# Two sets of PSUM evictions move from VectorE to ScalarE in a fused performer-attention and mixer kernel

## The chip, the cores and the metric

The kernel runs on one core of a Trainium2 chip. The metric is the device time of one execution in microseconds (us); the time before is the median of three runs. Everything about where time goes is read from one profiled execution, taken by the hardware profiler. Engines are called as in the profile: PE is TensorE, DVE is VectorE, ACT is ScalarE, POOL is GpSimd, SP is SyncE.

## The reference

Eight batches of eight heads with 576 rows of 64 go through a linear attention with random features, and its output goes through a mixer over tokens and then over channels:

```python
def phi(x):                                   # x: q or k, scaled
    h = einsum('bhsd,md->bhsm', x, omega) - sum(x * x) / 2
    return exp(h - max(h)) / sqrt(m)          # 128 features
kv  = einsum('bhsm,bhsd->bhmd', phi(k), v);  z = sum(phi(k), axis=2)
num = einsum('bhsm,bhmd->bhsd', phi(q), kv)
den = einsum('bhsm,bhm->bhs', phi(q), z) + 1e-06
x = (num / den).transpose(0, 2, 1, 3).reshape(8, 576, 512)
u = x + (relu(x.T @ w_tok1) @ w_tok2).T       # token mixing, 576 -> 256 -> 576
out = u + relu(u @ w_ch1) @ w_ch2             # channel mixing, 512 -> 1536 -> 512
```

## The kernel before

**Tiling.** The 576 rows of a batch are split into a main part of 512 rows (four blocks of 128) and a tail of 64 rows. The tails of two batches share one tile of 128 partitions: `xt[0]` and `xt[1]` hold the normalised tails of alternate pairs of batches, batch b using partitions `(b % 2) * 64` onward. In the profile the two are `xt`.

**Attention, per pair of heads (hp).** `t_main` and `t_tail` (L174, L185) transpose q and k on PE; DVE copies the result out (qT, kT at L182, tailT at L193). `q_proj` and `k_proj` (L241, L252) multiply by omega, and ACT takes the exponential out of PSUM (q_p, k_p, k_pt, q_pt, all at L197). `k_max` (L267) finds each row's maximum of k_p on DVE (mx L270, km L274, reciprocal v_sc L278) and POOL scales v with it (L279). `kv` (L286) accumulates five matmuls, and ACT casts the result to kv_sb (L301). `num` (L304) makes, for one head, a PSUM tile num_ps with five blocks of 65 columns: four main blocks and one tail block, the last column of each being the denominator. Then DVE takes the reciprocal of the denominators (rc, L317), multiplies the four main blocks into the batch's tile xm (L318), and multiplies the tail block into xt (L325).

**Token mixing.** `tok1` (L334) multiplies the four main blocks (L339) and then the shared tail tile xt (L342) by w_tok1; the half of the weight tile that belongs to the other batch of the pair is zero, so the matmul reads all of xt. Its relu is on ACT for the first half (L346) and on DVE for the second (L348). `tok2` (L350) adds the residual on DVE (um, L358), and `u_transpose` (L375) transposes the sum on PE and copies it on DVE (uT, L379).

**Channel mixing.** `ch1` (L387) makes twelve blocks of 128 channels: four matmuls (L393) and a relu into r3. Two of three relus are on ACT (L403); those of blocks 2, 5, 8 and 11 (`cb % 3 == 2`) are on DVE (L401). `ch2` (L405) accumulates twelve matmuls (L408), DVE adds the residual (o_sb, L417) and SP stores it.

**Order.** The scheduler is off: each engine runs its instructions in the order in which the program issues them, and that order is one list sorted by hand-written places (`at`, L168; `spread`, L465). A pair of heads takes one unit. Attention of batch b lies at places 4b to 4b+4, its token mixing at about 4(b+1)+0.85 to +3.85, its channel mixing at 4(b+2) to 4(b+3). So three batches are in flight, and channel mixing begins when two batches of attention are done. Within a unit, the relus of `ch1` and the exponentials stand in one queue on ACT, and the work of `k_max`, `num`, `tok2`, `u_transpose` and `ch2` in one queue on DVE. `num` of a pair stands behind `k_max` of the next pair.

**Buffers.** PSUM has eight banks: five for attention tiles (`att_ps`) and three for the mixer's (`mix_ps`). A matmul that opens a tile waits until the bank's former tile has been read.

Of the kernel before, what the change touches and what calls it, by code (L numbers as in the profile page):

```python
# [11 lines left out]
AF = mybir.ActivationFunctionType  # L12
ALU = mybir.AluOpType
# [4 lines left out]
def kernel(  # L18
# [17 lines left out]
    nc = tc.nc  # L36

    B, H, S, D = q.shape
# [6 lines left out]
    ST = S - SM  # L45
    NJ = SM // P
# [14 lines left out]
    def att_ps(shape, dt, name):  # L61
        return pspool.tile(shape, dt, name=name, tag="attps", bufs=5)

    def mix_ps(shape, dt, name):
        return pspool.tile(shape, dt, name=name, tag="mixps", bufs=3)
# [105 lines left out]
    live = {}  # L171
# [132 lines left out]
    def num(b, hp, i):  # L304
        h = 2 * hp + i
        if h == 0:
            live["x", b] = mpool.tile([P, NJ, DM], FP16, name="xm", tag="xm")
        sb = live["kv", b, h]
        ps = att_ps([P, NJ + 1, D + 1], FP32, "num_ps")
        for j in range(NJ):  # L310
            nc.tensor.matmul(  # L311
                ps[:, j, :], live["qp", b, hp][:, j % 2, 2 * i + j // 2, :], sb, start=True, stop=True
            )
        c0 = ST + (h % 2) * 256 + hp * ST - (b % 2) * ST
        nc.tensor.matmul(ps[:, NJ, :], q_pt[b % 2][:, c0 : c0 + P], sb, start=True, stop=True)
        rc = apool.tile([P, NJ + 1], FP32, name="rc", tag="rc")
        nc.vector.reciprocal(out=rc, in_=ps[:, :, D])  # L317
        nc.vector.tensor_tensor(  # L318
            out=live["x", b][:, :, h * D : (h + 1) * D],
            in0=ps[:, 0:NJ, 0:D],  # L320
            in1=rc[:, 0:NJ].unsqueeze(2).broadcast_to((P, NJ, D)),
            op=ALU.mult,
        )
        r0 = (b % 2) * ST
        nc.vector.tensor_scalar(  # L325
            out=xt[(b // 2) % 2][r0 : r0 + ST, h * D : (h + 1) * D],
            in0=ps[r0 : r0 + ST, NJ, 0:D],
            scalar1=rc[r0 : r0 + ST, NJ : NJ + 1],
            scalar2=None,
            op0=ALU.mult,  # L330
        )


# [53 lines left out]
    def ch1(c, cb):  # L387
        if cb == 0:
            live["r3", c] = mpool.tile([P, NCB, SM], FP16, name="r3", tag="r3")
        uT = live["uT", c] if c < B else uTt  # L390
        ps = mix_ps([P, SM], FP32, "h3_ps")
        for db in range(ND):
            nc.tensor.matmul(  # L393
                ps,
                wc1[:, db, cb * P : (cb + 1) * P],
                uT[:, db].rearrange("p j c -> p (j c)"),
                start=(db == 0),
                stop=(db == ND - 1),
            )
        if cb % 3 == 2:  # L400
            nc.vector.tensor_relu(out=live["r3", c][:, cb, :], in_=ps)  # L401
        else:
            nc.scalar.activation(out=live["r3", c][:, cb, :], in_=ps, func=AF.Relu)  # L403

    def ch2(c, j):  # L405
        ps = mix_ps([P, DM], FP32, "h2_ps")
# [35 lines left out]
    for b in range(B):  # L442
        g = 4 * b
        at(g - 0.95, t_main, b, 0, "q")
        at(g - 0.80, t_main, b, 0, "k")
        at(g - 0.45, t_tail, b)
        at(g - 0.20, q_tail, b)
        at(g + 0.40, k_tail, b, 0)
        at(g + 0.50, k_tail, b, 1)
        at(g + 0.70, k_tail_max, b)  # L450
        at(g + 1.02, t_main, b, 1, "q")
        at(g + 1.70, t_main, b, 1, "k")
        for hp in range(NU):
            u = g + hp
            at(u + 0.04, q_proj, b, hp, 0)
            at(u + 0.10, q_proj, b, hp, 1)
            at(u + 0.18, k_proj, b, hp, 0)
            at(u + 0.26, k_proj, b, hp, 1)
            at(u + 0.55, k_max, b, hp)
            at(u + 1.32, kv, b, hp, 0)  # L460
            at(u + 1.40, kv, b, hp, 1)
            at(u + 1.58, num, b, hp, 0)
            at(u + 1.66, num, b, hp, 1)
# [18 lines left out]
    for c in range(B + 1):  # L482
        items = [(4, ch1, c, cb) for cb in range(NCB)] + [(12, ch2, c, j) for j in range(NJ)]
        spread(4 * (c + 2), 4 * (c + 3), items)
# [33 lines left out]
```

## Time and profile before

| | |
|---|---|
| three runs | 357.69, 357.98 and 358.46 us, median 357.98 |
| the profiled execution | 357.74 us, of which the span from first to last instruction is 355.9 us |
| PE | 314.9 us busy, 88% of the span |
| DVE | 215.7 us busy, 61%, 523 instructions |
| ACT | 138.1 us busy, 39%, 297 instructions |
| POOL | 88.8 us busy, 25% |
| granted TensorE clock | 0.987 of full speed, mean |

The span falls into three parts. Up to about 61 us there is attention of two batches, with PE busy little more than half of the time. From 61 to 281 us come six stages of about 36 us, one per batch of channel mixing, with attention, token mixing and channel mixing interleaved and PE nearly always busy. From 281 us on there is little but channel mixing left. A line of a group gives engine, line, what is written from what, the count, and after the bar the busy time, the mean duration in ns and the idle time before. A row of the stretches gives the stretch, its length, and then per engine busy time with the number of instructions, the granted clock and the DMA's share.

### The profile page before, as it was taken

What the parts mean: (1) busy time and instruction counts of PE and PEld (TensorE: products, weight loads), DVE (VectorE), ACT (ScalarE), POOL (GpSimd) and SP (SyncE); (2) the same over time, 40 slices, a digit from 0 to 9 for tenths busy, and PEclk for the clock granted to TensorE, in tenths of its full rate; (3) what the DMA queues carried; (4) which work ended last, traced back from release to release, by engine and by line L of the source; (5) the groups of instructions that cost most, each with busy time, mean ns of one, the idle gap of its engine ahead of it and who ended that gap; (6) DMA issues with size and microseconds to landing.
All of it is one profiled execution on the core that took longest, in us unless ns stands there. A gap on an engine that the chain in (4) does not pass through costs nothing.

```text
span 355.9 us, 5929 instructions
## 1 busy us (share of the span) xinstructions
PE 314.9 (88%) x2337; PEld 171.8 (48%) x2337; DVE 215.7 (61%) x523; ACT 138.1 (39%) x297; POOL 88.8 (25%) x106
## 2 busy tenths in 40 slices
PE   2546784999999998999999989999999899999994
PEld 1334352555654564556554645555545444444441
DVE  3457788377767685777676857776767645322221
ACT  1325742553265226532653256425642140040410
POOL 8787362125013500261126112111211100000000
PEclk9999998799999999999999999999999999999998
DMA  7999999009700960099009900011001100201113
GB/s 72 164 191 210 205 192 188 10 0 145 146 30 2 148 141 29 3 112 177 30 2 115 174 29 2 15 47 62 0 2 59 61 0 29 88 3 62 58 29 89
DMA packets 45916, 27.78 MB, mean 78 GB/s; under 512 B 14144, under 2 KB 40640, under 8 KB 45888
## 3 DMA queue, kind: packets, MB, share of 16 engines
q0 software_dynamic: 40640, 17.96, 40.3%
q1 hardware_dynamic: 5248, 9.44, 7.6%
q8 instruction: 18, 0.29, 0.3%
q14 instruction: 10, 0.08, 0.1%
HBM read 35.91 MB, written 9.44 MB: 127 GB/s over the span
## 4 chain that ended last, share of the span: by engine, by line
PE 68%; DVE 20%; POOL 3%; issue 3%; DMA 3%; ACT 2%; DVEq 0%; ACTq 0%; POOLq 0%
PE h_ps L393 26%; PE h_ps L408 21%; PE k_ps L258 3%; DVE xm L318 3%; DVE km L274 3%; PE h_ps L339 3%; PE ht_ps L355 3%; PE q_ps L247 3%; DMA w1m<-in_moe_w_tok_dram 3%; PE t_ps L180 2%; DVE xt L325 2%; DVE mx L270 2%; DVE uT L379 2%; PE kv_ps L290 2%; DVE um L358 2%
## 5 line engine op out<-in xcount | busy, mean ns | idle before, releaser
L393 PE MATMUL h_ps<-uT,wc 128*128 128x512 f16 x384 | 95.9, 384 | 7.3 <-DVE uT L379 7.2
L408 PE MATMUL h_ps<-wc,r 128*128 128x512 f16 x432 | 98.1, 379 | 0.5 <-DVE ut L373 0.3
L279 POOL TENSOR_TENSOR v_sc<-v_nat,v_sc 128x512 f16<-128x512 f16 x32 | 34.0, 1062 | 168.2 <-DVE rc L317 103.1
L403 ACT ACTIVATE r<-h_ps 128x512 f16<-128x512 f32 x72 | 43.1, 598 | 79.8 <-PE h_ps L393 79.8
L393 PEld LDWEIGHTS <-wc 128*128 128x128 f16 x432 | 40.3, 98 | 50.0 <-issue 13.2
L408 PEld LDWEIGHTS <-r 128*128 128x128 f16 x432 | 41.3, 98 | 46.2 <-issue 1.1
L401 DVE TENSOR_SCALAR r<-h_ps 128x512 f16<-128x512 f32 x36 | 24.8, 690 | 58.7 <-PE h_ps L393 58.5
L197 ACT ACTIVATE q_p<-q_ps 128x512 f16<-128x512 f32 x64 | 37.0, 595 | 50.6 <-PE q_ps L247 49.9
L197 ACT ACTIVATE k_p<-k_ps 128x512 f16<-128x512 f32 x64 | 37.9, 602 | 26.4 <-PE k_ps L258 26.4
L417 DVE TENSOR_TENSOR o_sb<-um,h_ps 128x512 f32<-128x512 f16 x32 | 21.9, 684 | 38.4 <-PE h_ps L408 38.2
L318 DVE TENSOR_TENSOR xm<-num_ps,rc 128x256 f16<-128x256 f32 x64 | 27.2, 424 | 2.2
L258 PE MATMUL k_ps<-bd,kT 128*128 128x256 f16 x128 | 25.6, 291 | 0.7 <-ACT q_p L197 0.3
L247 PE MATMUL q_ps<-qT,bd 128*128 128x512 f16 x64 | 24.4, 407 | 0.0
L358 DVE TENSOR_TENSOR um<-xm,ht_ps 128x512 f16<-128x512 f16 x32 | 21.8, 681 | 2.0 <-PE ht_ps L355 1.5
L274 DVE TENSOR_REDUCE km<-mx 128x8 f16<-128x512 f16 x32 | 22.0, 686 | 1.1
L258 PEld LDWEIGHTS <-kT 128*128 128x128 f16 x128 | 12.9, 104 | 16.6 <-issue 3.5
L311 PEld LDWEIGHTS <-q_p 128*128 128x128 f16 x256 | 15.3, 98 | 10.5 <-issue 4.0
L290 PEld LDWEIGHTS <-k_p 128*128 128x128 f16 x256 | 14.2, 101 | 12.5 <-issue 8.2
L290 PE MATMUL kv_ps<-v_sc,k_p 128*128 128x65 f16 x256 | 15.4, 197 | 5.3 <-POOL v_sc L279 5.1
L355 PE MATMUL ht_ps<-r,w2m 128*128 128x512 f16 x64 | 19.0, 379 | 0.1
L311 PE MATMUL num_ps<-kv_sb,q_p 128*128 128x65 f16 x256 | 17.3, 194 | 1.9 <-ACT kv_sb L301 1.7
L325 DVE TENSOR_SCALAR xt<-num_ps,rc 64x64 f16<-64x64 f32 x64 | 17.8, 279 | 0.5
(81 smaller groups left out, 363.4 us busy)
## 6 DMA issues: line engine op xcount, KB each, us to landing
out_dram<-o_sb SPq DMA_DIRECT2D x32, 256.0 KB, 2.3
v_nat<-in_v_dram POOLq DMA_DIRECT2D x8, 512.0 KB, 10.4
q_nat<-in_q_dram POOLq DMA_DIRECT2D x7, 512.0 KB, 5.9
k_nat<-in_k_dram POOLq DMA_DIRECT2D x7, 512.0 KB, 8.4
wc<-in_moe_w_ch_dram POOLq DMA_DIRECT2D x2, 1536.0 KB, 18.2
out_dram<-o_sb SPq DMA_DIRECT2D x8, 128.0 KB, 2.3
qk_tail<-in_q_dram POOLq DMA_DIRECT2D x8, 64.0 KB, 8.0
qk_tail<-in_k_dram POOLq DMA_DIRECT2D x8, 64.0 KB, 8.2
```

The costliest lines, as they stand in the source:

```text
L197: nc.scalar.activation(out=out, in_=in_, func=AF.Exp, bias=0.0, scale=c_scale)
L247: nc.tensor.matmul(ps, bd[:, w * M : (w + 1) * M], sb[:, i0 : i0 + 4, :], start=True, stop=True)
L258: nc.tensor.matmul(ps[:, 2 * pr : 2 * pr + 2, :], sb[:, (hp % 2) * 4 + 2 * i + pr, :], bd, start=True, stop=True,)
L274: nc.vector.reduce_max(out=mx, in_=tmp, axis=AX.X)
L279: nc.gpsimd.tensor_tensor(out=vs[:, :, 0:D], in0=nat["v", b][:, 2 * hp : 2 * hp + 2, :].rearrange("p h (j d) -> p (h j) d", d=D), in1=vs[: ...
L290: nc.tensor.matmul(ps, live["kp", b, hp][:, i, j, :], live["vsc", b, hp][:, i * 4 + j, 0 : D + 1], start=(j == 0), stop=False,)
L311: nc.tensor.matmul(ps[:, j, :], live["qp", b, hp][:, j % 2, 2 * i + j // 2, :], sb, start=True, stop=True)
L318: nc.vector.tensor_tensor(out=live["x", b][:, :, h * D : (h + 1) * D], in0=ps[:, 0:NJ, 0:D], in1=rc[:, 0:NJ].unsqueeze(2).broadcast_to((P, ...
L355: nc.tensor.matmul(ps, w2m[:, tb, j, :], live["r1", b][:, tb, :], start=(tb == 0), stop=(tb == NT - 1))
L393: nc.tensor.matmul(ps, wc1[:, db, cb * P : (cb + 1) * P], uT[:, db].rearrange("p j c -> p (j c)"), start=(db == 0), stop=(db == ND - 1),)
L403: nc.scalar.activation(out=live["r3", c][:, cb, :], in_=ps, func=AF.Relu)
L408: nc.tensor.matmul(ps, live["r3", c][:, cb, j * P : (j + 1) * P], wc2[:, cb, :], start=(cb == 0), stop=(cb == NCB - 1),)
```

## The change

Two evictions from PSUM change engine. In `num`, the multiplication of the tail block by the reciprocal (64 partitions, 64 columns, one per head, 64 in all) becomes an ACT activation with the function Copy and the reciprocal as a scale per partition. In `ch1`, the relu of every third block becomes an ACT activation like the others (four per batch and stage, nine stages, 36 in all). Nothing else is edited; places, tiles and buffers stay.

```diff
     # num(b, hp, i)
-        nc.vector.tensor_scalar(
+        nc.scalar.activation(
             out=xt[(b // 2) % 2][r0 : r0 + ST, h * D : (h + 1) * D],
-            in0=ps[r0 : r0 + ST, NJ, 0:D],
-            scalar1=rc[r0 : r0 + ST, NJ : NJ + 1],
-            scalar2=None,
-            op0=ALU.mult,
+            in_=ps[r0 : r0 + ST, NJ, 0:D],
+            func=AF.Copy,
+            scale=rc[r0 : r0 + ST, NJ : NJ + 1],
         )
     # ch1(c, cb)
-        if cb % 3 == 2:
-            nc.vector.tensor_relu(out=live["r3", c][:, cb, :], in_=ps)
-        else:
-            nc.scalar.activation(out=live["r3", c][:, cb, :], in_=ps, func=AF.Relu)
+        nc.scalar.activation(out=live["r3", c][:, cb, :], in_=ps, func=AF.Relu)
```

DVE's queue goes from 525 rows to 425. In the first place shown, DVE stands in the second stage of channel mixing, where block 8 has been multiplied and the first two heads of the next batch (num_ps 1557 and 1573) are being normalised; h3_ps is the PSUM tile of a ch1 block, h1_ps that of tok1. Before:

```order
L401 TENSOR_SCALAR r3_1373<-h3_ps_1543 128x512
L270 TENSOR_TENSOR mx_1549<-k_p_1504 128x512
L274 TENSOR_REDUCE km_1551<-mx_1549 128x8
L278 RECIPROCAL v_sc_1553<-km_1551 128x8
L317 RECIPROCAL rc_1563<-num_ps_1557 128x5
L318 TENSOR_TENSOR xm_1556<-num_ps_1557,rc_1563 128x4x64
L325 TENSOR_SCALAR xt1_110<-num_ps_1557,rc_1563 64x64
L317 RECIPROCAL rc_1579<-num_ps_1573 128x5
L318 TENSOR_TENSOR xm_1556<-num_ps_1573,rc_1579 128x4x64
L325 TENSOR_SCALAR xt1_110<-num_ps_1573,rc_1579 64x64
L182 COPY kT_1592<-t_ps_1583 128x1024
L348 TENSOR_SCALAR r1_1509<-h1_ps_1600 128x512
```

The same place on DVE now:

```order
L270 TENSOR_TENSOR mx_1549<-k_p_1504 128x512
L274 TENSOR_REDUCE km_1551<-mx_1549 128x8
L278 RECIPROCAL v_sc_1553<-km_1551 128x8
L317 RECIPROCAL rc_1563<-num_ps_1557 128x5
L318 TENSOR_TENSOR xm_1556<-num_ps_1557,rc_1563 128x4x64
L317 RECIPROCAL rc_1579<-num_ps_1573 128x5
L318 TENSOR_TENSOR xm_1556<-num_ps_1573,rc_1579 128x4x64
L182 COPY kT_1592<-t_ps_1583 128x1024
L347 TENSOR_SCALAR r1_1509<-h1_ps_1600 128x512
```

The relu ahead of the maximum and the two tail rows are gone; the rest keeps its order.

At the same place ACT has the exponentials of a pair of heads, the relu of tok1 (r_1509) and relus of ch1 (r_1373). Before:

```order
L197 ACTIVATE k_p<-k_ps 128x512
L346 ACTIVATE r_1509<-h_ps 128x512
L403 ACTIVATE r_1373<-h_ps 128x512
L197 ACTIVATE k_p<-k_ps 128x512
L301 CAST kv_sb<-kv_ps 128x65 x2
L403 ACTIVATE r_1373<-h_ps 128x512 x2
L197 ACTIVATE q_p<-q_ps 128x512 x2
```

And now:

```order
L197 ACTIVATE k_p<-k_ps 128x512
L345 ACTIVATE r_1509<-h_ps 128x512
L399 ACTIVATE r_1373<-h_ps 128x512
L197 ACTIVATE k_p<-k_ps 128x512
L301 CAST kv_sb<-kv_ps 128x65 x2
L399 ACTIVATE r_1373<-h_ps 128x512
L325 ACTIVATE xt_110<-num_ps,rc 64x64
L399 ACTIVATE r_1373<-h_ps 128x512
L325 ACTIVATE xt_110<-num_ps,rc 64x64
L399 ACTIVATE r_1373<-h_ps 128x512 x2
L197 ACTIVATE q_p<-q_ps 128x512 x2
```

The relus of blocks 8 and 11 have come in, and the two tail rows stand between relus, so that a relu behind a tail row waits for what the tail row waits for.

The last place is on ACT in the stretch before any channel mixing, where the fourth pair of heads of the first batch ends and the second batch begins (q_pt is the tail of q). Before:

```order
L197 ACTIVATE k_p<-k_ps 128x512 x2
L301 CAST kv_sb<-kv_ps 128x65 x2
L197 ACTIVATE q_pt_117<-qt_ps 128x512
L197 ACTIVATE q_p<-q_ps 128x512 x2
L197 ACTIVATE k_p<-k_ps 128x512 x2
```

And now:

```order
L197 ACTIVATE k_p<-k_ps 128x512 x2
L301 CAST kv_sb<-kv_ps 128x65 x2
L325 ACTIVATE xt_109<-num_ps,rc 64x64 x2
L197 ACTIVATE q_pt_117<-qt_ps 128x512
L197 ACTIVATE q_p<-q_ps 128x512 x2
L197 ACTIVATE k_p<-k_ps 128x512 x2
```

Two tail rows now stand ahead of the next pair's five exponentials. In the built program the tail row on ACT waits for DVE's xm (L318) of the same head, which reads the same PSUM tile, and not only for the reciprocal.

## The prediction, made before the change was run

> **What bounds the kernel now.** I read the table of stretches first, cut at the starts of the channel-mixing stages. Columns are the stretch and its length, then the busy time of PE, weight load, DVE, ACT and POOL with counts, granted clock, DMA share, GB/s.
>
> ```profile
> 41.00:61.20 20.20, 11.95 (x139) 7.90 (x139) 18.23 (x46) 7.74 (x19) 8.93 (x10) 0.96 1.52 194
> 61.20:99.30 38.10, 38.05 (x284) 20.91 (x284) 24.56 (x62) 15.95 (x35) 9.97 (x11) 0.93 0.52 75
> 99.30:136.40 37.10, 34.64 (x277) 19.50 (x277) 26.49 (x63) 17.15 (x38) 9.96 (x11) 1.00 0.49 77
> 136.40:171.90 35.50, 35.48 (x284) 20.02 (x284) 24.47 (x62) 15.74 (x35) 9.98 (x11) 1.00 0.52 81
> 171.90:209.00 37.10, 34.65 (x277) 19.50 (x277) 26.49 (x63) 17.16 (x38) 9.96 (x11) 1.00 0.50 77
> 209.00:244.50 35.50, 35.47 (x284) 20.02 (x284) 24.47 (x62) 15.75 (x35) 5.28 (x5) 1.00 0.08 31
> 244.50:280.90 36.40, 33.52 (x254) 18.15 (x254) 24.95 (x60) 15.96 (x36) 5.28 (x5) 1.00 0.08 30
> 309.40:351.00 41.60, 41.49 (x193) 18.58 (x190) 11.30 (x18) 9.55 (x16) 0.00 (x0) 1.00 0.16 49
> ```
>
> Stages 1, 3 and 5 and the end are PE from edge to edge: what leaves DVE there is worth nothing. PE idles about 2.5 us in stages 2 and 4 (37.10 - 34.64) and 2.9 us in stage 6. From 41 to 61 us DVE is the fullest engine, 18.23 of 20.2 us.
>
> Next, whom PE waits for, first around stage 2, then around the end of stage 6 (total, times, longest):
>
> ```profile
> PE h_ps L393 <- DVE uT L379: 1.7, 1, 1.7
> PE h_ps L342 <- DVE xt L325: 0.7, 1, 0.7
> ...
> PE h_ps L393 <- DVE uT L379: 1.8, 1, 1.8
> PE h_ps L342 <- DVE xt L325: 0.7, 1, 0.7
> PE uT_ps L378 <- DVE o_sb L417: 0.3, 1, 0.3
> ```
>
> Stage 4 has the same two waits as stage 2. All end on DVE, one on the very instruction that moves. The chain that ended last shows what stands ahead of both waits of stage 2 (start, duration):
>
> ```profile
> 111.71 0.69 DVE r L401
> 112.43 0.44 DVE mx L270
> ...
> 114.42 0.29 DVE xt L325
> ...
> 114.97 0.42 DVE xm L318
> ...
> 115.75 0.38 PE h_ps L342
> ...
> 130.73 0.69 DVE um L358
> ...
> 133.65 0.29 DVE xt L325
> ...
> 133.97 0.42 DVE uT L379
> ...
> 134.97 0.29 DVE xt L325
> ...
> 135.29 0.69 DVE o_sb L417
> ...
> 136.37 1.02 PE h_ps L393 x4
> ```
>
> The first chain begins with a ch1 relu, which holds DVE until PE has made its block, and runs through both tail rows to tok1's last matmul. The second begins when PE has made the input of um and runs through two tail rows to the transposed sum that opens the next stage.
>
> **The change, part by part.** The prices, from the groups:
>
> ```profile
> L403 ACT ACTIVATE r<-h_ps 128x512 f16<-128x512 f32 x72 | 43.1, 598 | 79.8 <-PE h_ps L393 79.8
> L401 DVE TENSOR_SCALAR r<-h_ps 128x512 f16<-128x512 f32 x36 | 24.8, 690 | 58.7 <-PE h_ps L393 58.5
> L325 DVE TENSOR_SCALAR xt<-num_ps,rc 64x64 f16<-64x64 f32 x64 | 17.8, 279 | 0.5
> L301 ACT CAST kv_sb<-kv_ps 128x65 f16<-128x65 f32 x64 | 11.8, 236 | 8.6 <-PE kv_ps L297 8.2
> ```
>
> DVE loses 36 x 0.690 + 64 x 0.279 = 42.7 us and goes from 215.7 to about 173. ACT gains 36 x 0.598 = 21.5 us plus 64 tail rows. No row shows a tail row on ACT; the cast of 65 columns (0.236) and the relu of 512 (0.598) bound it. I take 0.24, from the cast, which has nearly the same width: 15 us, so ACT comes to about 175 of 355 us. The Trainium skill (ScalarE: Activation LUTs, "What ACT_TABLE_LOAD costs") gives 186 ns + 0.833 ns per element plus 93 ns for a pointer operand, by which I estimate 0.33 us; by that every tail row below comes 0.09 us later and the sum stays.
>
> *tok1's wait, stages 2, 4 and 6.* PE's timeline (start, duration):
>
> ```profile
> 113.17 1.03 PE L393 MATMUL h_ps<-uT,wc 128*128 128x512 f16 x4
> 114.04 1.03 PE L339 MATMUL h_ps<-xm,w1m 128*128 128x512 f16 x4
> 115.75 0.38 PE L342 MATMUL h_ps<-xt,w1t 128*128 128x512 f16 x1 [0.69 <-DVE xt L325]
> ```
>
> Four matmuls take 114.04 - 113.17 = 0.87 us of PE, so the tail matmul could start at 114.91 and starts 0.84 us late. ACT's timeline tells when DVE may start now:
>
> ```profile
> 110.81 0.59 ACT L197 ACTIVATE k_p<-k_ps 128x512 f16<-128x512 f32 x1
> 112.78 0.60 ACT L403 ACTIVATE r<-h_ps 128x512 f16<-128x512 f32 x1 [1.15 <-PE h_ps L393]
> ```
>
> k_p is done at 111.40; mx started at 112.43 only because the relu stood ahead. So mx moves up 1.0 us, and the first tail row gives back its slot of 0.3 us ahead of the second xm, which ended at 115.39 and now ends at about 114.1. The tail row follows on ACT, 0.05 us of hand-over and 0.24 us: 114.4, half a microsecond before PE wants it. At 0.598 it is 114.75, still in time. Gain 3 x 0.84 = 2.5 us.
>
> What queues behind ACT's waits there: block 9's relu, 112.78 before, now stands behind the first tail row, whose xm ends at 113.4, so it runs at 113.7 to 114.3. Its bank is wanted again three mixer tiles later, by block 11 at about 115.1. That is my cover, 0.8 us; the rival below takes it away.
>
> *The wait that opens stages 3, 5 and 7.* From um at 130.73 everything is DVE back to back, with two tail-row slots: 133.65 to 133.97 and 134.97 to 135.29, 0.32 us each. Both go; um still waits for PE, so nothing else moves, and 1.0 us of the wait stays. Gain 3 x 0.64 = 1.9 us. The short wait in stage 6, 0.3 us behind o_sb, has two such slots ahead of it and goes: 0.3 us.
>
> *The first 61 us.* Here PE, ACT and DVE hand work round, and the new waits act. Three rows of ACT and DVE, and the tail rows of 41 to 61.2 us alone:
>
> ```profile
> 35.71 0.60 ACT L197 ACTIVATE q_pt<-qt_ps 128x512 f16<-128x512 f32 x1 [1.25 <-PE qt_ps L203]
> ...
> 36.12 0.42 DVE L318 TENSOR_TENSOR xm<-num_ps,rc 128x256 f16<-128x256 f32 x1
> ...
> 38.30 0.43 DVE L270 TENSOR_TENSOR mx<-k_p 128x512 f16<-128x512 f16 x1 [1.57 <-ACT k_p L197]
> ...
> 41.00:61.20 20.20, 1.94 (x7) 0.96 1.52 194
> ```
>
> q_pt and four exponentials stood ahead of the second xm; now they wait for it (36.54), for DVE running some 0.3 us later there by the same kind of wait one pair earlier, and for the tail row: 37.15 instead of 35.71. So k_p, and with it mx at 38.30, comes 1.4 us late. After that DVE is nearly full and loses the slots of the last row (tail rows from 41 to 61.2 us: seven, 1.94 us). The lag is absorbed as far as DVE had queued work. Ends: -1.9 us (slots regained, no lag) and +1.4 us (lag kept). I take 0, as they nearly cancel.
>
> *Relus elsewhere.* At the end a block comes every 0.87 us and ACT needs 0.60: covered by PE. The same holds from 281 us on. In stages 1, 3 and 5 both edits lie under a full PE.
>
> Sum: 2.5 + 1.9 + 0.3 = 4.7 us, 357.74 - 4.7 = 353.0 for an execution like the profiled one, which lies 0.24 us under the median of the runs; on the median 353.3 us. A measurement of this kernel tells about 0.2% (0.7 us) from no change.
>
> **The rivals.**
>
> *Head of line on ACT (slower).* In each of seven stages two pairs of heads lie among relus, 14 places. If the chain from k_p's end to the second xm takes over 0.8 us more than I reckon, a relu behind a tail row frees its bank too late and PE stops in every stage, the full ones too. At 0.5 us per place it costs 7 us: 360.3. It decides from 4.7 / 14 = 0.34 us per place. For it: the strict queue on ACT and three banks. Against: chain rows that add up to 2.7 us with the slots out, and a DVE with idle time there (58.7 us ahead of L401). 0.08.
>
> A second way to the slow side: the Trainium skill (ScalarE: Activation LUTs, "Rules for kernel authors") has relu belong on VectorE, up to three times faster per element in bf16. Were that so here, an ACT relu would take 3 x 0.69 = 2.1 us, and the 24 relus of the last two ch1 stages, one per 0.87 us, would add 24 x 1.2 = 29 us: 382. The rows, 598 against 690 ns from the same f32 PSUM, say the opposite: 0.01.
>
> *tok1's wait stays.* The tail row comes late on ACT, say behind a relu that waits for PE, and the 2.5 us are not had: 355.8. For it: only half a microsecond of slack. 0.10.
>
> *The start keeps its lag and goes cold.* The clock was halved before stage 1:
>
> ```profile
> 59.20:66.20 7.00, 4.97 (x19) 2.19 (x19) 1.86 (x6) 2.97 (x7) 0.25 (x1) 0.53 0.80 91
> ```
>
> 5 us of matmul ran there at about half clock, 2.5 us lost, after PE had been mostly idle. If ACT's waits thin out PE earlier as well and this comes once more, 353.3 + 1.4 + 2.5 = 357.2. The Trainium skill (TensorE: Matmul & The Clock Gate, "What's actually happening") tells the same: half clock after an idle window of about 3.4 us, full after a busy one. The trace agrees with 0.53. Against: before 61 us PE is seldom the last. 0.08.
>
> *Nothing to gain.* Another DVE wait takes the place of each that goes: 358.0. Against: the rows ahead of both waits are one engine back to back. 0.04.
>
> **How the numbers follow.** Forecast 0.69, at 353.3; its own ends are -1.9 and +1.4, 351.4 to 354.7. With tok1's wait staying (355.8) and half the cold start taken in, the range is 351.6 to 356.3. Faster by over 0.2%: forecast, tok1's wait, half the cold start, 0.83. Within 0.2%: the other half and nothing to gain, 0.08. Slower: 0.09.
>
> **What would show it.** Right: no PE wait on xt at L342 in stages 2, 4 and 6; the uT wait ahead of stages 3, 5 and 7 at about 1.0 us; stages 2 and 4 at 35.6 us, 3 and 5 unchanged; PE still full at the end; first ch1 matmul between 59.3 and 62.6 us. Wrong: PE waits on an ACT relu (L399) or on a bank within stages 3 and 5; L342 waiting for ACT; the tail row on ACT over 0.6 us; a first ch1 matmul after 63 us or a second cold stretch.

## The result, and the profile after

The changed kernel takes 348.11 us (median of four runs, 347.84 to 348.58) against 358.22 us for the kernel before beside it (four runs): a ratio of 0.972, 95% interval 0.970 to 0.974. A second comparison, made later with six and eleven runs, gave 349.28 against 357.23 us, 0.977 (0.974 to 0.980). The direction was forecast, the size was not: 348.11 lies under the range's low end of 351.6. The profiled execution took 348.58 us with a span of 346.8 us, 9.1 us less span than before.

First the busy times of the changed kernel and its two groups of moved instructions, from the page and the groups:

```profile
PE 310.2 (89%) x2337; PEld 170.4 (49%) x2337; DVE 176.3 (51%) x423; ACT 173.5 (50%) x397; POOL 89.0 (26%) x106
```

```profile
L399 ACT ACTIVATE r<-h_ps 128x512 f16<-128x512 f32 x108 | 64.3, 601 | 46.2 <-PE h_ps L392 45.3
...
L325 ACT ACTIVATE xt<-num_ps,rc 64x64 f16<-64x64 f32 x64 | 19.7, 309 | 63.4 <-DVE xm L318 33.8 <-DVE rc L317 25.2 <-PE q_ps L247 2.8
```

DVE came to 176.3 us (about 173 forecast), ACT to 173.5 (about 175). The relu costs what the others cost, 601 ns, against 690 ns on DVE; so the rule of the Trainium skill that relu belongs on VectorE (ScalarE: Activation LUTs, "Rules for kernel authors"), whose figure is for bf16, does not hold for this f32 PSUM source. The tail row takes 309 ns where I took 240; the estimate of 0.33 us from the Trainium skill (ScalarE: Activation LUTs, "What ACT_TABLE_LOAD costs") was the nearer one.

The table of stretches, cut at the starts of the stages as before (busy time of PE, weight load, DVE, ACT, POOL, then granted clock):

```profile
60.90:96.20 35.30, 35.30 (x284) 20.00 (x284) 20.75 (x50) 20.66 (x48) 9.98 (x11) 1.00 0.58 82
96.20:131.50 35.30, 34.48 (x277) 19.47 (x276) 21.30 (x51) 20.97 (x50) 9.98 (x11) 1.00 0.52 81
131.50:166.90 35.40, 35.35 (x284) 20.05 (x284) 20.77 (x50) 20.24 (x49) 9.99 (x11) 1.00 0.52 81
...
237.60:271.70 34.10, 33.06 (x255) 18.12 (x254) 19.65 (x48) 20.31 (x48) 5.29 (x5) 1.00 0.09 32
```

PE's idle time in stage 2 fell from 2.5 to 0.8 us and in stage 6 from 2.9 to 1.0 us. Stage 1 shows a granted clock of 1.00, where before had 0.93, and PE did its work there in 35.3 instead of 38.05 us. PE's waits around stage 2 are now a single one:

```profile
PE h_ps L392 <- DVE uT L378: 0.8, 1, 0.8
```

The wait of tok1 on xt is gone, in stages 2, 4 and 6; the wait that opens stages 3, 5 and 7 is 0.81, 0.81 and 0.92 us (about 1.0 forecast).

From the first `ch1` matmul of each stage in PE's timeline (60.87, 96.22, 131.55, 166.90 us and so on) comes the account of the 9.1 us:

| place | forecast | measured, profile before to after |
|---|---|---|
| start up to stage 1 | 0 | 61.23 to 60.87: -0.36 |
| stage 1 | 0 | 38.11 to 35.35: -2.76 |
| stage 2 | -1.48 | 37.03 to 35.33: -1.70 |
| stage 3 | 0 | 35.57 to 35.35: -0.22 |
| stage 4 | -1.48 | 37.02 to 35.32: -1.70 |
| stage 5 | 0 | 35.57 to 35.35: -0.22 |
| stage 6 | -1.78 | 36.34 to 34.10: -2.24 |
| stage 7 and end | 0 | 75.0 to 75.1: +0.1 |
| sum | -4.74 | -9.1 |

So stages 2 to 6 gave 6.1 us where 4.74 were forecast, and 2.8 us came from stage 1, where I had forecast nothing. What follows asks about both.

### The profile page after: what moved, and what is told of

It is laid out like the page before. It is cut to its first block, busy times and chain, and to the rows that moved or that the text cites. A ratio compares the mean times of both kernels' runs of the same rounds, so it can differ in the third digit from the quotient of the medians.

```text
span 346.8 us, 5958 instructions
## 1 busy us (share of the span) xinstructions
PE 310.2 (89%) x2337; PEld 170.4 (49%) x2337; DVE 176.3 (51%) x423; ACT 173.5 (50%) x397; POOL 89.0 (26%) x106
## 3 DMA queue, kind: packets, MB, share of 16 engines
HBM read 35.91 MB, written 9.44 MB: 131 GB/s over the span
## 4 chain that ended last, share of the span: by engine, by line
PE 77%; DVE 9%; ACT 4%; POOL 4%; DMA 3%; issue 2%; DVEq 0%; ACTq 0%; POOLq 0%
PE h_ps L392 27%; PE h_ps L404 25%; PE h_ps L338 3%; PE k_ps L258 3%; PE ht_ps L354 3%; PE q_ps L247 3%; PE t_ps L180 3%; DMA w1m<-in_moe_w_tok_dram 3%; PE num_ps L311 2%; DVE xm L318 2%; PE kv_ps L290 2%; DVE km L274 2%; ACT k_p L197 1%; ACT q_p L197 1%; PE uT_ps L377 1%
## 5 line engine op out<-in xcount | busy, mean ns | idle before, releaser
L392 PE MATMUL h_ps<-uT,wc 128*128 128x512 f16 x384 | 94.2, 379 | 3.7 <-DVE uT L378 3.7
L399 ACT ACTIVATE r<-h_ps 128x512 f16<-128x512 f32 x108 | 64.3, 601 | 46.2 <-PE h_ps L392 45.3
L325 ACT ACTIVATE xt<-num_ps,rc 64x64 f16<-64x64 f32 x64 | 19.7, 309 | 63.4 <-DVE xm L318 33.8
L270 DVE TENSOR_TENSOR mx<-k_p 128x512 f16<-128x512 f16 x32 | 13.5, 422 | 51.9 <-ACT k_p L197 51.9
L318 DVE TENSOR_TENSOR xm<-num_ps,rc 128x256 f16<-128x256 f32 x64 | 27.2, 425 | 2.4 <-DVE rc L317 0.2
L258 PE MATMUL k_ps<-bd,kT 128*128 128x256 f16 x128 | 24.9, 284 | 2.2 <-ACT xt L325 2.2
L247 PE MATMUL q_ps<-qT,bd 128*128 128x512 f16 x64 | 23.7, 395 | 0.0
(80 smaller groups left out, 350.1 us busy)
```

Of the source, the lines that this page charges most:

```text
L247: nc.tensor.matmul(ps, bd[:, w * M : (w + 1) * M], sb[:, i0 : i0 + 4, :], start=True, stop=True)
L258: nc.tensor.matmul(ps[:, 2 * pr : 2 * pr + 2, :], sb[:, (hp % 2) * 4 + 2 * i + pr, :], bd, start=True, stop=True,)
L318: nc.vector.tensor_tensor(out=live["x", b][:, :, h * D : (h + 1) * D], in0=ps[:, 0:NJ, 0:D], in1=rc[:, 0:NJ].unsqueeze(2).broadcast_to((P, ...
L392: nc.tensor.matmul(ps, wc1[:, db, cb * P : (cb + 1) * P], uT[:, db].rearrange("p j c -> p (j c)"), start=(db == 0), stop=(db == ND - 1),)
```

## The experiments

All are compared with the kernel before, run beside them (median 357.39, 357.23 and 357.82 us in the three sessions).

**The two halves of the change.** One kernel moves only the tail rows (the first hunk of the change's diff), one only the relus (the second hunk). For the tail rows alone:

> Only the tail rows move to ScalarE, the ch1 relus stay split. Theory (the cold stretch after 59 us of before is gone because the tail rows change the first 61 us; a tail-row slot on VectorE is worth 0.42 us and not 0.32): the first 61 us are as in the changed kernel, first ch1 matmul at 60.9 us and at full clock, uT waits ahead of stages 3, 5, 7 at 0.8 us, tok1's wait at about 0.4 us since the relu still holds VectorE; about 351 us. Rival (stage 1 gets shorter because the relus leave VectorE there): stage 1 stays at 38 us, about 353.5 us.

Measured 352.99 us (350.89 to 353.34, four runs), ratio 0.986 (0.982 to 0.990). For the relus alone:

> Only the ch1 relus move to ScalarE, the tail rows stay on VectorE. Theory: the first 61 us are those of before, with the half clock from 59 to 66 us; tok1's wait goes (3 x 0.84 us), the uT waits stay at 1.7 us; about 355.5 us. Rival: stage 1 falls from 38.1 to about 35.4 us, about 353 us.

Measured 354.65 us (354.12 to 354.98, four runs), ratio 0.992 (0.989 to 0.995). PE's waits over the whole execution (total, times, longest), in before, then with the tail rows moved, then with the relus moved:

```profile
PE h_ps L393 <- DVE uT L379: 7.2, 4, 2.1
PE h_ps L342 <- DVE xt L325: 2.9, 4, 0.8
```

```profile
PE h_ps L392 <- DVE uT L378: 3.7, 4, 1.2
PE h_ps L341 <- ACT xt L325: 3.1, 4, 0.8
```

```profile
PE h_ps L393 <- DVE uT L379: 7.2, 4, 2.0
PE h_ps L342 <- DVE xt L325: 0.8, 1, 0.8
```

Each half takes away or shortens one of the two waits and leaves the other. tok1's wait (three times 0.75 us in the stages, and one at the start) stays with the tail rows on ACT and goes with the relus: it was the relu ahead of mx. The wait for uT (7.2 us over four places) falls to 3.7 us with the tail rows: it was their slots. The forecast's two causes were right. That the tail rows alone would end the half clock was wrong: both profiles still have a spell of it (a stretch with the granted clock at half) in stage 1, which is 36.96 and 37.21 us long, against 35.35, though the tail-row kernel has the same 1.19 us wait ahead of stage 1 as the changed kernel. So the clock was a question of its own.

**The clock out of the way.** Seventeen matmuls that nobody reads, put ahead of stage 1, in before and in the changed kernel:

```diff
+    def warm(n):
+        if "warm" not in live:
+            live["warm"] = mix_ps([P, SM], FP32, "warm_ps")
+        for _ in range(n):
+            nc.tensor.matmul(
+                live["warm"], ident16, w1m[:, 0:2, :].rearrange("p j t -> p (j t)"), start=True, stop=True
+            )
+    at(7.70, warm, 4)
+    at(7.79, warm, 5)
+    at(8.06, warm, 8)
```

In before:

> The kernel before, with 17 extra matmuls of 512 columns into a bank that nobody reads, put where PE waits between 56 and 61 us. Theory: PE no longer idles, the clock is not halved, stage 1 takes 35.6 us and not 38.1 us, the start stays or moves by under 0.5 us; about 355.7 us. Rival (the half clock is not what stage 1 costs): 358 us or more.

Measured 355.44 us (353.58 to 355.73, five runs), ratio 0.993 (0.990 to 0.996): matmuls that do nothing make the kernel before 2 us faster. In the changed kernel:

> The changed kernel with the same 17 extra matmuls; the control. Theory: there is no cold stretch to save, so 348.1 to 348.8 us. Rival (extra matmuls help in some way other than the clock): about 2 us less than the changed kernel.

Measured 348.88 us (347.82 to 349.18, four runs): the matmuls bring the changed kernel nothing. These are the rows of the stretches that cover the start of stage 1, in before and then in before with the extra matmuls:

```profile
60.20:63.60 3.40, 2.37 (x7) 0.91 (x7) 0.93 (x3) 0.47 (x1) 0.00 (x0) 0.50 1.13 134
63.60:67.00 3.40, 3.40 (x22) 1.92 (x21) 0.00 (x0) 2.42 (x8) 0.00 (x0) 0.58 0.00 0
```

```profile
60.20:63.60 3.40, 3.08 (x27) 1.85 (x26) 0.36 (x1) 1.93 (x4) 0.00 (x0) 1.00 0.97 113
63.60:67.00 3.40, 3.40 (x27) 1.79 (x26) 2.22 (x6) 2.61 (x8) 0.11 (x1) 1.00 0.00 0
```

The clock is at 1.00, and stage 1 takes 35.57 instead of 38.11 us: 2.54 us of stage 1's 2.76 are the clock, the other 0.22 is the same as in stages 3 and 5. With the clock kept at stage 1 in both kernels the change is worth 355.44 - 348.88 = 6.56 us by the medians, and by stages 1 to 6 of the two profiles 217.1 - 210.8 = 6.3 us.

**Does the changed kernel keep its clock?** The same kernel once more, and a variant in which PE waits longer ahead of stage 1:

> The changed kernel as it is, once more. The first experiments left one thing open: the half-clock spell at the first channel-mixing stage is in the profiles of before and of both halves of the change, and not in those of the changed kernel. Theory A (the PE wait that opens stage 1, 2.05 us before and 1.19 us now, triggers it): the changed kernel never has it, all runs lie within 347.5 to 349 us. Theory B (the clock looks at windows whose phase differs from run to run, and the stretch from 57 to 61 us is thin enough for a half clock in some phases): some runs lie about 2 us higher, near 350.5 us, with a lower granted clock, as the four runs of the tail-rows-only kernel did (350.9 to 353.3). I give A 0.4, B 0.6, since that kernel went cold with the same 1.19 us wait.

The six runs fall into two groups: 348.13, 348.22 and 348.48 us, and 350.07, 350.07 and 350.39 us. The profiled one is of the second group. Its stretches around the start of stage 1, and then those of the first profile of the very same kernel:

```profile
56.80:60.20 3.40, 1.47 (x21) 1.00 (x19) 3.19 (x10) 0.31 (x1) 1.05 (x1) 1.00 1.65 187
60.20:63.60 3.40, 2.90 (x10) 1.30 (x10) 0.45 (x2) 2.97 (x6) 0.00 (x0) 0.68 1.11 127
63.60:67.00 3.40, 3.40 (x30) 2.03 (x29) 1.26 (x4) 2.47 (x7) 0.00 (x0) 0.82 0.06 5
```

```profile
56.80:60.20 3.40, 1.62 (x23) 1.13 (x21) 3.19 (x10) 0.41 (x2) 1.05 (x1) 1.00 1.68 186
60.20:63.60 3.40, 2.73 (x24) 1.62 (x24) 0.61 (x2) 3.00 (x7) 0.00 (x0) 1.00 1.12 131
63.60:67.00 3.40, 3.40 (x31) 1.91 (x28) 2.28 (x7) 2.98 (x9) 0.89 (x1) 1.00 0.01 0
```

The same program with the same waits lost (0.32 + 0.18) x 3.4 = 1.7 us of clock in one profile and nothing in the other, and stage 1 was 37.03 us long in one and 35.35 in the other. Theory B stands. The half-clock time is (0.32 + 0.18) x 3.4 x 2 = 3.4 us; summed over half-microsecond stretches, every spell from 12 to 70 us of which the profiles record both ends comes to 3.4, 6.8 or 10.2 us, so the half clock goes in steps of 3.4 us. That is what the Trainium skill says (TensorE: Matmul & The Clock Gate, "What's actually happening"): the clock is set by windows of 3413 ns that run freely and do not start with the kernel, and the trace agrees. With a longer wait:

```diff
-    def u_transpose(src, dst):
+    def u_transpose(src, dst, n=1):
...
-        nc.vector.tensor_copy(out=dst, in_=ps)
+        for _ in range(n):
+            nc.vector.tensor_copy(out=dst, in_=ps)
...
-        u_transpose(live["u", b][:, j, :], live["uT", b][:, :, j, :])
+        u_transpose(live["u", b][:, j, :], live["uT", b][:, :, j, :], 3 if (b, j) == (0, 3) else 1)
```

> The changed kernel with the copy of the transposed sum that PE waits for ahead of stage 1 made three times, so that this wait grows by two copies of 0.43 us from 1.19 to 2.05 us, its length in before. That alone costs 0.9 us: 349.0 to 349.2 us. Theory A (the length of this wait triggers the half clock): stage 1 is 2.5 us longer in the profile and in most runs, 351.5 us. Theory B (phase of the windows): 349.1 us in most runs, with more runs near 351.5 than the unchanged copy beside it has.

Measured 350.88 us, all five runs between 350.20 and 351.17; 0.86 us more than the quick group of the kernel beside it would be 349.1 us, and none is there. The profile of this one has the wait at 2.1 us and stage 1 at 37.85 us:

```profile
PE h_ps L393 <- DVE uT L379: 4.7, 4, 2.1
```

```profile
56.80:60.20 3.40, 0.78 (x4) 0.39 (x4) 3.02 (x10) 1.68 (x4) 1.05 (x1) 0.72 1.69 186
60.20:63.60 3.40, 3.40 (x10) 1.37 (x9) 0.00 (x0) 1.59 (x4) 0.00 (x0) 0.50 0.85 97
```

That is what theory A forecast for most runs. So both seem to play: how idle PE is ahead of stage 1 changes how often the half clock comes (three of ten runs of the changed kernel, taking both comparisons, and all five of this one by their times), and the phase, that is where the windows begin, decides in the single run. Two runs of the changed kernel and one of this one were profiled; for the rest the spell is read from the time.

The profiles show how the two work together, when PE's busy time is summed over stretches of 3.41 us laid end to end from the edges of the recorded spells. Ahead of the spell at stage 1, PE was busy for 0.99 us of such a stretch in before, for 1.32 us in the second profile of the changed kernel and for 1.73 us with the longer wait. In the first profile of the changed kernel an edge lies at 58.99 us, in the second at 58.02. So in the first the idle time ahead of stage 1 is split between two stretches, which are busy for 2.20 and 2.13 us, and no spell follows. None follows in the kernels with the extra matmuls either, where these stretches are busy for 2.74 us or more. In before and with the longer wait the next stretch, at half clock already, was busy for only 1.80 and 1.73 us, and the spell lasted 6.8 us instead of 3.4. These figures give no threshold: earlier in the profile of the doubled rows below, a stretch with 1.91 us was followed by half clock and one with 1.60 us was not.

**The last wait.** In the changed kernel the uT copies that PE waits for stand behind a head's normalisation. The last transpose of an even batch goes ahead of it:

```diff
-        items += [(1, tokT, b, 2), (1, tokT, b, 3)]
+        items += [(1, tokT, b, 2)]
+        if b % 2:
+            items += [(1, tokT, b, 3)]
+        else:
+            at(4 * (b + 1) + 3.65, tokT, b, 3)
+            items += [(1, lambda: None)]
```

> The changed kernel with the last transpose of an even batch (and its copy on DVE) moved ahead in the order, in front of the normalisation of the head that stood between it and um. Theory (what is left of the wait that opens stages 3, 5 and 7, 0.8 to 0.9 us, is DVE's queue between um and the copy): these waits go, 3 x 0.8 = 2.5 us, less what PE then waits elsewhere in the same place, about 1 us each: 345.3 to 347 us. Rival (PE waits the same time at the transposes, which now need um sooner, since um itself waits for PE): 348.2 us, with PE's wait at the transpose rows for um.

Measured 347.08 us (346.50 to 347.85, five runs), just over the forecast's 345.3 to 347 and 2.2 us under the median of the unchanged kernel beside it, which lies between that kernel's two groups; stages 2 to 6 of the profiles differ by 1.75 us. Its waits of PE:

```profile
PE h_ps L392 <- DVE uT L378: 0.6, 1, 0.6
PE uT_ps L377 <- DVE um L357: 0.6, 3, 0.2
```

Ahead of stages 3, 5 and 7 the wait for uT is gone, and 0.2 us at the transpose is what it leaves, less than the 1 us that I had put down. Stages 2, 4 and 6 are 34.70, 34.69 and 33.38 us, stages 3 and 5 35.46. Stage 1 of its profile has one spell of half clock and takes 37.04 us.

**The cover on ACT.** Every tail row twice:

```diff
-        nc.scalar.activation(
+        for _ in range(2):
+            nc.scalar.activation(
...
```

> The changed kernel with every tail row issued twice on ACT: 64 more ACT instructions of 0.31 us, two more per pair of heads, in the same places. It tests the cover that the prediction named (0.8 us from a relu behind a tail row to the matmul that wants its bank). Theory (the cover holds): the stages stay at 35.35 us, at most 1 us more at the start, where the exponentials wait: 348.2 to 349.5 us. Rival (head of line on ACT is close): relus behind the tail rows come 0.3 to 0.6 us later, PE stops for a bank in every stage at 14 places, 352 us or more.

Measured 353.22 us (352.43 to 355.65, six runs): 3.9 us over the kernel beside it, the rival's number without its mechanism. Stages 2, 4 and 6 are 35.92, 35.91 and 34.69 us, each 0.6 us longer; stages 3 and 5 are 35.44, only 0.1 longer. PE stops at one place in each even stage, not at 14 places: tok1's wait is back, on ACT now.

```profile
112.76 0.65 ACT L326 ACTIVATE xt<-num_ps,rc 64x64 f16<-64x64 f32 x2 [1.20 <-DVE rc L317]
113.43 0.60 ACT L400 ACTIVATE r<-h_ps 128x512 f16<-128x512 f32 x1
114.05 0.65 ACT L326 ACTIVATE xt<-num_ps,rc 64x64 f16<-64x64 f32 x2
```

```profile
113.30 1.03 PE L339 MATMUL h_ps<-xm,w1m 128*128 128x512 f16 x4
114.76 0.38 PE L342 MATMUL h_ps<-xt,w1t 128*128 128x512 f16 x1 [0.43 <-ACT xt L326]
```

In the two profiles the stretch up to stage 1 differs by 61.61 - 60.70 = 0.9 us, the even stages make 1.8, and the profiled runs differ by 2.86 us; the rest of the 3.9 us between the medians lies in the runs' spread.

**The halves again, without the clock,** each with the seventeen matmuls. Tail rows:

> Tail rows alone moved, with the 17 matmuls that keep PE busy ahead of stage 1, so that the clock does not enter. Against 355.44 us of the kernel before with these matmuls. Theory (each tail row out of DVE is worth a slot of 0.42 us on PE's path, and tok1's relu wait on DVE stays): stages 2 and 4 36.23 us, stage 6 35.00 us, together 2.9 us less: 352.5 us. Rival (the tail rows' gain in the run without these matmuls was clock): above 354 us.

Measured 352.33 us (351.32 to 353.09, four runs); stages 2, 4 and 6 at 36.22, 36.22 and 34.99 us. Relus:

> Relus alone moved, with the same 17 matmuls. Theory (tok1's wait goes because mx no longer stands behind a relu; the wait that opens stages 3, 5 and 7 keeps its 1.7 us): stages 2, 4 and 6 0.85 us shorter each, 2.6 us less than 355.44: 352.9 us. The two halves then give 2.9 + 2.6 = 5.5 of the 6.6 us between 355.44 and 348.88 us, the rest from stages 3 and 5 and the start, where both are needed. Rival (their gain was clock): above 354 us.

Measured 351.93 us (351.68 to 352.80, four runs); the same stages at 36.17, 36.18 and 35.49 us. Against 355.44 us the halves give 3.1 and 3.5 us, together 6.6, and the whole gives 6.56. That they seem to add up is chance: the halves ran in another session, beside a kernel before that took 0.43 us more, and their runs lie up to 1.8 us apart. By stages 1 to 6 of the profiles the halves give 2.8 and 2.5 us and the whole 6.3, so 1.0 us needs both, as this expectation had it. Most of it lies in stages 1, 3 and 5: tail rows alone 35.63 us, relus alone 35.57, both 35.35.

**The early transpose with the extra matmuls:**

> The changed kernel with the last transpose of an even batch moved ahead and with the 17 matmuls ahead of stage 1: the best of what the runs point to. The early transpose took 0.65 us from stages 2, 4 and 0.7 from stage 6, gave back 0.1 in 3 and 5, and began stage 1 some 1 us sooner; the matmuls take away the half clock at stage 1 (1.7 us in its profile): 345.5 to 346.8 us, and all runs within 1 us of each other. Rival (the matmuls delay the first stage as much as the clock cost): 347 us or more.

Measured 347.57 us (346.62 to 347.91, five runs). The rival's figure: stage 1 is down from 37.04 to 35.36 us, but begins at 61.61 instead of 59.36 us. How much of that is the matmuls and how much the half clock earlier on, these two profiles don't tell. The early transpose alone, 347.08 us, is the quickest kernel of the study; between these two the runs show no difference.

## Why the direction was right and the size wrong

**tok1's wait, 3 x 0.84 us: right, with less room than said.** It went as forecast, and for the reason given. But the second tail row came nearly too late. ACT's and PE's timelines of the changed kernel in stage 2:

```profile
110.39 0.31 ACT L325 ACTIVATE xt<-num_ps,rc 64x64 f16<-64x64 f32 x1 [1.20 <-DVE rc L317]
110.73 0.60 ACT L399 ACTIVATE r<-h_ps 128x512 f16<-128x512 f32 x1
111.35 0.31 ACT L325 ACTIVATE xt<-num_ps,rc 64x64 f16<-64x64 f32 x1
```

```profile
110.93 1.03 PE L338 MATMUL h_ps<-xm,w1m 128*128 128x512 f16 x4
111.79 0.38 PE L341 MATMUL h_ps<-xt,w1t 128*128 128x512 f16 x1
```

The row ends at 111.66, and PE takes it at 111.79. That is 0.13 us, of which the hand-over takes about 0.06 (with the doubled rows, from 114.70 to 114.76), and not half a microsecond. I let the row follow its xm at 114.1, though by my own working the relu between the two rows ran until 114.3; in fact ACT was in it until 111.33. The doubled rows, which bring the end 0.34 us later at the first and 0.34 at the second, lost 0.6 us per even stage, as a slack of 0.07 makes of 0.68.

**The wait that opens stages 3, 5 and 7, 3 x 0.64 us: the mechanism right, the slot mis-sized.** Two slots of 0.32 us were to go; the wait shrank by 0.86 us (1.67 to 0.81). DVE's timeline, before and after:

```profile
133.21 0.42 DVE L318 TENSOR_TENSOR xm<-num_ps,rc 128x256 f16<-128x256 f32 x1
133.65 0.29 DVE L325 TENSOR_SCALAR xt<-num_ps,rc 64x64 f16<-64x64 f32 x1
133.97 0.42 DVE L379 COPY uT<-uT_ps 128x512 f16<-128x512 f16 x1
```

```profile
129.25 0.43 DVE L318 TENSOR_TENSOR xm<-num_ps,rc 128x256 f16<-128x256 f32 x1
129.59 0.41 DVE L378 COPY uT<-uT_ps 128x512 f16<-128x512 f16 x1
```

From xm to uT it was 0.76 us and is 0.34: a tail row cost 0.42, because xm itself held DVE 0.44 us ahead of a tail row and holds it 0.34 ahead of a copy. I had read only the distance from the tail row to what came next. Worth 3 x 0.22 = 0.7 us.

That price is not one for all tail rows. In the profile of before, all 32 tail rows of the odd batches, on partitions 64 to 127, start 0.44 to 0.46 us after their xm, when its bar of 0.42 has ended, and a ready instruction on all partitions starts 0.32 us after them, when their bar of 0.29 has ended. All 32 of the even batches, on partitions 0 to 63, start 0.34 us after their xm, and such an instruction starts 0.19 us after them, under a bar of 0.27. So a slot of an odd batch costs 0.42 us and one of an even batch 0.34 + 0.19 - 0.34 = 0.19 us; the two slots that the forecast read belong to an odd batch. What costs is the change of the first partition: mxt (L226), on partitions 64 to 127 in every batch, starts 0.21 us after an odd batch's tail row, under its bar, and 0.30 us after an even batch's, when its bar has ended.

**"In stages 1, 3 and 5 both edits lie under a full PE": wrong by 0.22 us each.** PE's timeline at the end of stage 3, before and after:

```profile
171.50 0.38 PE L247 MATMUL q_ps<-qT,bd 128*128 128x512 f16 x1
171.94 1.02 PE L393 MATMUL h_ps<-uT,wc 128*128 128x512 f16 x4
```

```profile
166.69 0.38 PE L247 MATMUL q_ps<-qT,bd 128*128 128x512 f16 x1
166.90 1.03 PE L392 MATMUL h_ps<-uT,wc 128*128 128x512 f16 x4
```

From start to start (the pitch) a matmul of 512 columns holds PE for about 0.21 us there, though its bar is 0.38 long; before, the next came 0.44 us later. PE waited 0.22 us under the end of that bar. DVE's timeline of before names for whom, a uT copy from 171.48 that ends at 171.89 behind two more tail rows:

```profile
171.29 0.27 DVE L325 TENSOR_SCALAR xt<-num_ps,rc 64x64 f16<-64x64 f32 x1
171.48 0.41 DVE L379 COPY uT<-uT_ps 128x512 f16<-128x512 f16 x1
```

A stretch whose PE is busy from edge to edge can thus hold a wait. That stages 3 and 5 need both halves of the change for this, the runs show. With the relus alone the tail rows still stand ahead of the uT copy. With the tail rows alone (and the extra matmuls) the end of stage 3 does gain its 0.22 us, but PE loses 0.28 us earlier, 0.21 of it in one stop: a tail row on ACT starts at 148.93 when DVE has made its input, the relu behind it ends at 149.73, and the ch1 matmul that the chain of that profile puts behind this relu starts at 149.77. With both halves nothing stops there, since mx no longer waits on DVE behind a relu and the tail row starts 1.0 us sooner relative to PE's matmuls.

**Stage 6: 2.24 us for 1.78.** 0.21 of the difference is the slots, and 0.25 is the short wait behind o_sb, forecast at 0.3. In PE's timeline of before the four transposes start 0.66 us after the k_proj matmuls ahead of them (270.84 to 271.50) and the next ch2 matmul 0.33 us after the transposes; in the changed kernel both distances are 0.22. That is 0.55 us, part of it under a bar as above.

**The first 61 us: 0 taken, -0.36 measured, the replay right.** ACT's queue at the place that the forecast spoke of, then DVE's:

```profile
37.05 0.31 ACT L325 ACTIVATE xt<-num_ps,rc 64x64 f16<-64x64 f32 x1 [0.25 <-DVE xm L318]
37.26 0.58 ACT L197 ACTIVATE q_pt<-qt_ps 128x512 f16<-128x512 f32 x1
```

```profile
39.79 0.43 DVE L270 TENSOR_TENSOR mx<-k_p 128x512 f16<-128x512 f16 x1 [2.84 <-ACT k_p L197]
```

q_pt was forecast at 37.15 and came at 37.26, mx was forecast 1.4 us late and came 1.5 late (38.30 to 39.79), and by 61 us nothing was left of it. How far -0.36 is the change and how far the clock can't be said. The stage began anywhere between 59.36 and 61.87 us in the eleven experiments. Ahead of the first change of the clock that a profile records, between 13.6 and 28.9 us, the rows print 1.00, but the pitch of 512 columns is 0.43 us there, twice the later one; counted as half, the half-clock time from 12 to 42 us lies between 9 and 19 us, with 16.9 us in before and 12.9 in the changed kernel.

**The step that failed most: the half clock at stage 1.** The prediction put it in a rival, as something that could come a second time. It did not ask what the change does to the spell that was there, and the sum put stage 1 at nothing, with a reason for DVE and none for the clock. With the change, PE waits 1.19 us ahead of stage 1 instead of 2.05, and the spell of 6.8 us was gone in one profile and 3.4 us long in the other. In the profile that the forecast is measured by, that is 2.54 of the 4.4 us that the spans fell further than forecast (9.1 against 4.7). The rest is 0.4 for the slots of stages 2 and 4, 0.7 for the hidden waits of stages 1, 3 and 5, 0.5 for stage 6 and 0.3 for the start and the end. The 5.2 us between 353.3 and 348.11 are these and 0.8 us from setting profiled runs against medians. Part of the gain is luck of that comparison: by their times, none of its four runs lost clock at stage 1, and three of the next six did. With the clock kept at stage 1, the change gives 6.3 to 6.6 us, still more than the 4.7 forecast.

**The rivals.** Head of line on ACT as forecast, at 14 places, does not come even with doubled rows; a slack that thin exists at one place per even stage, the one that "tok1's wait stays" named. With the tail rows alone it stops PE at one place in each of stages 1, 3 and 5, for 0.2 us. "The start keeps its lag and goes cold" came true by half in the second profile of the changed kernel, with a spell that cost 1.7 us and no lag to see.

## What to carry to other kernels

Before pricing a wait, price the clock: where the granted clock is under 1 inside a stage that is otherwise full, ask whether the edit makes TensorE busier ahead of it, and compare kernels over enough runs to see both phases. The cost of a small instruction on a full engine is the difference between two distances, from the instruction ahead of it to the one behind it with and without it, not its busy time. A matmul's bar overlaps the next one's (0.38 us long, 0.21 from start to start here), so a wait shorter than that overlap shows only as a pitch that is too long.

## What the runs showed of the hardware that was not expected

- One and the same program ran in two groups of times 1.9 us apart (348.1 to 348.5 and 350.1 to 350.4 us). Its two profiles, of runs of 348.58 and 350.07 us, differ by one half-clock spell of 3.4 us where PE was full, which cost 1.7 us.
- Seventeen matmuls without a use made the kernel before 2 us faster (355.44 against 357.39 us), and brought nothing where the clock was mostly kept (348.88 against 348.11 and 349.28 us).
- On DVE the same xm instruction on all partitions, 0.42 us busy, held the engine at least 0.44 us ahead of a tail row on partitions 64 to 127 (32 of 32) and 0.34 us ahead of one on partitions 0 to 63 (32 of 32): in these rows and at mxt, an instruction that starts on another partition than the one ahead of it began only when that one's bar had ended. On ACT a ready relu started 0.33 us after a tail row on partitions 64 to 127 and 0.21 us after one on partitions 0 to 63 (bars of 0.31 us).
- The granted clock in the rows is 1.00 ahead of the first recorded change, up to 28.9 us in before, while matmuls of 512 columns ran there 0.43 us apart, against 0.21 later.
